# Two indirect gathers for w_out's last two rows a partition, and z computed in rows by 72 matmuls

## The chip, the core and the metric

The kernel runs on one core of a Trainium2 chip. The metric is the device time of one execution in microseconds (us), lower is better. Engines are named as the profile names them: PE (matmuls, with PEld for its weight loads), DVE (vector), ACT (activations and copies), POOL (GpSimd), SP (issues transfers). 16 DMA engines move the data.

## What is computed

One decoding step with one new token. The normalised row goes through attention over a window of 4096 keys and through a gated MLP; both are added to the input.

```
xn = layernorm(x)                                # x: 1 x 576
q  = xn @ wq                                     # 32 heads of 128
k, v = k_cache[:, -4096:], v_cache[:, -4096:]    # 16 heads of 128, each for two heads of q
A  = softmax(q k^T / sqrt(128)) v @ wo           # wo: 4096 x 576

z  = gelu(xn @ w_in)                             # w_in: 576 x 4608
z1, z2 = z[:2304], layernorm(z[2304:])
B  = (z1 * (w_sp * z2 + b_sp)) @ w_out           # w_out: 2304 x 576
out = x + A + B
```

All arrays are bfloat16. Keys, values and weights together are 51 MB, each byte of which is read once.

## The kernel before

**Loads.** SP issues every large load, in a fixed order, into four large buffers that are used in turn (tags a, b, c, d): wq in two parts, K of head groups 0 and 1, w_in in two parts (win, rest), K of group 2, V 0, K 3, V 1, V 2, V 3, then w_out (one load, line 106) and wo in five loads of 14, 9, 6, 2 and 1 rows a partition (line 108). A load waits until the tile that had its buffer before has been read. Four heads make a group; there are four groups. Partition p holds rows 18p to 18p+17 of w_out and 32 rows of wo.

**Order of work.** The order on every engine is written out by hand from line 420 on; nothing is rescheduled. For a group g and half c, `keys(g, c)` transposes the keys with four DVE instructions of 128x1024 (line 258, tile kT), and `scores(g, c)` multiplies them with q (line 265, 16 matmuls into S). `sm_a(g)` takes the maximum (line 286, mx), spreads it over the partitions and lets ACT take the exponential (line 292, pz). `sm_b(g)` transposes the result on DVE (line 303, pt) and copies it with 16 ACT instructions (line 306, PT). `sums(g)` and `pv(g)` are PE's (lines 312 and 329: 32 matmuls with V into ops). `tail(g)` normalises on DVE (rs, om, on), gathers the heads by four matmuls (line 350, yps) and copies them into Y (line 357). From line 426 the calls run: z_mms, sm_b(0), sm_a(1), keys and scores(2,0), sm_b(1), z_exp, keys and scores(2,1), ..., tail(2), sm_b(3), sums(3), pv(3), out_hv(0), out_hv(1), tail(3), out_hv(2), and the products with wo.

**The gated MLP.** `z_mms` (line 360) computes z with the weights as the stationary operand: for each of 9 slices of w_in and each of 18 columns t a weight load of 128x128 and a matmul whose moving operand is XT (two columns, one for each half of z): 162 weight loads and 162 matmuls. The result zps has z in columns: partition p, position t. `z_exp` copies it to SBUF (line 372) and starts the gelu, `z_gelu` ends it, and `z_norm` computes hv, of 18 columns, the factor of w_out; its power (line 404) is POOL's.

**The output.** `acc` has the two parts of the output row (264 and 312 columns) in two banks of PSUM. `out_mms` adds one row a partition of a weight: two matmuls, one for each part, with one column of hv or Y as the stationary operand. `out_hv(c)` does so for six of w_out's 18 rows. Y is complete after tail(3); then the 32 rows of wo follow in order of their loads. DVE and ACT each convert one part (lines 480 and 481), and ACT issues the store.

**Pools that the change touches.** Tag m of ps_m is one PSUM bank that small results use in turn (qps2, lps, psz, yps), so each of them waits until the one before has been read. Tag pt of `single` is the tile of sm_b. The PSUM tags a and b are acc's from line 436 on.

Of the kernel before, what the change touches and what calls it, by code (L numbers as in the profile page):

```python
# [7 lines left out]

FP32 = mybir.dt.float32
BF16 = mybir.dt.bfloat16  # L10
ALU = mybir.AluOpType
ACT = mybir.ActivationFunctionType
AXX = mybir.AxisListType.X

D = 576
# [12 lines left out]
NF = FH // 128  # L28
CUT = (0, 264, D)
XP = D // 3  # L30
EPS = 1e-5
SCALE = DH ** -0.5
GELU_C = 0.7978845608028654
NS = 9


@with_exitstack
def kernel(
# [14 lines left out]
    nc = tc.nc  # L53
    P = nc.NUM_PARTITIONS
# [5 lines left out]
    work = ctx.enter_context(tc.tile_pool(name="work", bufs=2))  # L60
    ktpool = ctx.enter_context(tc.tile_pool(name="ktpool", bufs=2))
    single = ctx.enter_context(tc.tile_pool(name="single", bufs=1))
    ps_s = ctx.enter_context(tc.tile_pool(name="ps_s", bufs=1, space=bass.MemoryType.PSUM))
    ps_o = ctx.enter_context(tc.tile_pool(name="ps_o", bufs=1, space=bass.MemoryType.PSUM))
    ps_m = ctx.enter_context(tc.tile_pool(name="ps_m", bufs=1, space=bass.MemoryType.PSUM))
    ps_a = ctx.enter_context(tc.tile_pool(name="ps_a", bufs=1, space=bass.MemoryType.PSUM))
    ps_b = ctx.enter_context(tc.tile_pool(name="ps_b", bufs=1, space=bass.MemoryType.PSUM))
# [6 lines left out]
    def rows(slot, src, name, lo, n, at=None):  # L74

        w = src.shape[1]
        if at is None:
            t = big.tile([P, n * w], BF16, name=f"{name}{lo}", tag=slot)[:]
        else:
            t = slot[:, at:at + n * w]  # L80
        v = t.rearrange("p (s c) -> p s c", c=w)
        nc.sync.dma_start(v, src.rearrange("(p s) c -> p s c", p=P)[:, lo:lo + n, :])  # L82
        return [(lo + s, v[:, s, :]) for s in range(n)]
# [19 lines left out]
    V[2] = load_kv("b", A_v_cache, 2, "v")  # L103
    V[3] = load_kv("c", A_v_cache, 3, "v")
    ends = [big.tile([P, TP * DH], BF16, name=f"end{n}", tag="ad"[n]) for n in range(2)]
    wout_sb = rows(ends[0], B_w_out, "wout", 0, NF, 0)
    wo_sb = []
    for n, t, at in ((14, 1, 0), (9, 1, 14), (6, 0, NF), (2, 0, NF + 6), (1, 0, NF + 8)):
        wo_sb += rows(ends[t], A_wo, "wo", len(wo_sb), n, at * D)
# [31 lines left out]
    for e in range(2):  # L141
# [5 lines left out]
                            axis=mybir.AxisListType.XY)  # L147
# [17 lines left out]
    for n in range(2):  # L165
        t = ps_s.tile([P, 2, 512], FP32, name=f"S{n}")
# [7 lines left out]
    lx = const.tile([P, NG], FP32, name="lx")  # L174
    mb = const.tile([P, 32], FP32, name="mb")
    nc.gpsimd.memset(mb[:], 0.0)

# [4 lines left out]
    for j in range(NS):  # L182
        nc.tensor.matmul(ps_x[:, j:j + 1], lhsT=xtw[:, j].rearrange("p m h -> p (m h)"), rhs=ones_b[:, 0:1],  # L183
                         start=True, stop=True)
# [6 lines left out]
        out=junk[:], in0=x_col[:], in1=x_col[:], scale=1.0, scalar=0.0,  # L191
# [13 lines left out]
    XT = const.tile([P, NS, 2], BF16, name="XT")  # L205
# [4 lines left out]
    nc.tensor.matmul(ps_x[:, 24:26], lhsT=ones_b[:], rhs=spb[:], start=True, stop=True)  # L210
    wb = const.tile([P, 2], FP32, name="wb")
    nc.vector.tensor_copy(wb[:], ps_x[:, 24:26])


    for s, wv in wq_sb:
        for g in range(4):
            nc.tensor.matmul(  # L217
                qps[32 * g:32 * g + 2, :], lhsT=XT[:, s, :], rhs=wv[:, 512 * g:512 * (g + 1)],
                start=(s == 0), stop=(s == NS - 1), tile_position=(0, 32 * g),
            )  # L220

    q_rep = const.tile([P, 8, 2, 4, 32], BF16, name="q_rep")
# [19 lines left out]
    for a in range(4):  # L242
        for h in range(2):
            for k2 in range(2):
                nc.vector.tensor_scalar_mul(qbv[:, a, h, k2], qpv[:, h, k2], mask4[:, a:a + 1])


    Y = const.tile([P, 32], BF16, name="Y")
    KT = {}
# [2 lines left out]
    def keys(g, c):  # L252

        kT = ktpool.tile([P, TC, 2, 8, GK, 2], BF16, name=f"kT{g}_{c}", tag="kT")
        src = K[g][:, TC * c:TC * (c + 1), :].rearrange("p t d -> p (t d)").bitcast(FP32)
        dst = kT[:].rearrange("p t b r x e -> p (t b r x e)").bitcast(FP32)
        for n in range(4):
            nc.vector.transpose(dst[:, 1024 * n:1024 * (n + 1)], src[:, 1024 * n:1024 * (n + 1)])  # L258
        KT[g, c] = kT

    def scores(g, c):
        kv = KT.pop((g, c))[:].rearrange("p (t s) b r x e -> p b e x t r s", s=2)
        for be in range(4):
            for x in range(GK):
                nc.tensor.matmul(  # L265
                    S[g % 2][32 * x:32 * x + 8, c, :],
                    lhsT=Qb[:, GK * g + x, be].rearrange("p a h -> p (a h)"),
                    rhs=kv[:, be // 2, be % 2, x],
                    start=(be == 0), stop=(be == 3), tile_position=(0, 32 * x),
                )  # L270
# [25 lines left out]
    def sm_b(g):  # L296
        pt = single.tile([P, TC, 32], FP32, name=f"pt{g}", tag="pt")
        src = pz[:].rearrange("p t r x e -> p (t r x e)").bitcast(FP32)
        dst = pt[:].rearrange("p t x -> p (t x)")
        PT = work.tile([P, TC, GK, 2, 2], BF16, name=f"PT{g}", tag="PT")  # L300
        PT4 = PT[:].rearrange("p t x h e -> p (t x h e)").bitcast(FP32).rearrange("p (t x h) -> p t x h", x=GK, h=2)
        for n in range(2):
            nc.vector.transpose(dst[:, 1024 * n:1024 * (n + 1)], src[:, 1024 * n:1024 * (n + 1)])  # L303
        for x in range(GK):
            for a in range(4):
                nc.scalar.copy(PT4[32 * a:32 * a + 32, :, x, :], pt[32 * x:32 * x + 32, :, 2 * a:2 * a + 2])  # L306
        st[g]["PT"] = PT

    def sums(g):

        lps = ps_m.tile([P, 32], FP32, name=f"lps{g}", tag="m")
        nc.tensor.matmul(lps[:, 0:1], lhsT=lsum[:].rearrange("p v y e -> p (v y e)"), rhs=lx[:, g:g + 1],
                         start=True, stop=True)
        st[g]["lps"] = lps
# [43 lines left out]


    def z_mms():  # L360
        zps = ps_a.tile([P, 2, NF], FP32, name="zps", tag="a")
        for s, wv in win_sb:
            wt = wv.rearrange("k (p t) -> k t p", t=NF)
            for t in range(NF):
                nc.tensor.matmul(zps[:, :, t], lhsT=wt[:, t, :], rhs=XT[:, s, :],  # L365
                                 start=(s == 0 and t == 0), stop=(s == NS - 1 and t == NF - 1),
                                 skip_group_check=True)
        return zps

    def z_exp(zps):  # L370
        z = const.tile([P, 2, NF], FP32, name="z")
        nc.vector.tensor_copy(z[:], zps[:])
        u = const.tile([P, 2, NF], FP32, name="u")
        nc.vector.tensor_mul(u[:], z[:], z[:])
        nc.vector.tensor_scalar(out=u[:], in0=u[:], scalar1=0.044715, scalar2=1.0,
                                op0=ALU.mult, op1=ALU.add)
        nc.vector.tensor_mul(u[:], u[:], z[:])
        th = const.tile([P, 2, NF], FP32, name="th")
        nc.scalar.activation(th[:], u[:], ACT.Exp, scale=-2.0 * GELU_C)
        return z, th  # L380
# [15 lines left out]
    def z_norm(G, sz):  # L396
        psz = ps_m.tile([P, 512], FP32, name="psz", tag="m")
        nc.tensor.matmul(psz[:, 0:2], lhsT=ones_f[:], rhs=sz[:], start=True, stop=True)
        mz = const.tile([P, 4], FP32, name="mz")
        nc.vector.tensor_scalar_mul(mz[:, 0:2], psz[:, 0:2], 1.0 / FH)  # L400
        nc.vector.tensor_mul(mz[:, 2:3], mz[:, 0:1], mz[:, 0:1])
        nc.vector.tensor_sub(mz[:, 2:3], mz[:, 1:2], mz[:, 2:3])
        nc.vector.tensor_scalar_add(mz[:, 2:3], mz[:, 2:3], EPS)  # L403
        nc.gpsimd.tensor_tensor(out=mz[:, 3:4], in0=mz[:, 2:3], in1=mhalf[:], op=ALU.pow)  # L404
        zn = const.tile([P, NF], FP32, name="zn")
        nc.vector.tensor_scalar(out=zn[:], in0=G[:, 1], scalar1=mz[:, 0:1], scalar2=mz[:, 3:4],
                                op0=ALU.subtract, op1=ALU.mult)
        nc.vector.tensor_scalar(out=zn[:], in0=zn[:], scalar1=wb[:, 0:1], scalar2=wb[:, 1:2],
                                op0=ALU.mult, op1=ALU.add)
        hv = const.tile([P, NF], BF16, name="hv")  # L410
        nc.vector.tensor_mul(hv[:], G[:, 0], zn[:])
        return hv
# [7 lines left out]
    for g in range(2):  # L420
        for c in range(2):
            keys(g, c)
            scores(g, c)
            if g == 1 and c == 0:
                sm_a(0)
    zps = z_mms()
    sm_b(0)
    sm_a(1)
# [24 lines left out]
    tail(1)  # L453
    sm_a(3)
    hv = z_norm(G, sz)
    sums(2)
    pv(2)
    tail(2)
    sm_b(3)
    sums(3)  # L460
    pv(3)

    def out_mms(lhs, col, wv, last):
        for n in range(2):
            nc.tensor.matmul(acc[n], lhsT=lhs[:, col:col + 1], rhs=wv[:, CUT[n]:CUT[n + 1]],  # L465
                             start=False, stop=last, tile_position=(0, 32 * n))
# [8 lines left out]
    out_hv(2)  # L475
    for t, wv in wo_sb:
        out_mms(Y, t, wv, t == 31)

    res = const.tile([1, D], BF16, name="res")
    nc.vector.tensor_copy(res[:, 0:CUT[1]], acc[0])  # L480
# [32 lines left out]
```

## Time and profile before

| | |
|---|---|
| Time, median of 3 runs (lowest to highest) | 126.92 us (126.77 to 126.95) |
| The profiled execution: its time, its span | 126.89 us, 125.1 us |
| Busy share of the span: PE, PEld, DVE, ACT, POOL | 57%, 23%, 63%, 34%, 6% |
| SP's queue: packets, data, share of 16 DMA engines | 2592, 50.96 MB, 95.2% |
| z: 126 + 36 matmuls on PE | 48.82 to 56.79 and 56.66 to 59.03 us |
| Last part of wo issued, then landed, as the chain of waits has it | 90.41 us, 121.27 us |
| Conversion of the result on ACT | 122.72 to 123.13 us |

The span runs from the first to the last instruction that the profile shows; the time of an execution has 1.8 us more around it. Times in the text are us from the start of the span. A line of the timeline has the start, the length, the engine, the line of code, the operation, the tiles written and read with their shapes, and the number of instructions put together; in brackets stands how long the engine was idle before and what ended that. A queue's line has its packets, megabytes, and the time of its packets as a share of 16 engines' span. The queue called q1 is SP's, q10 is ACT's, and q8 and q14 bring instructions to the engines.

### The profile page before, as it was taken

Reading aid. Unit: us, or ns where it says so; the run is one execution under the profiler, and the core shown is the slowest. Engines: PE = TensorE matmul, PEld = TensorE weight load, DVE = VectorE, ACT = ScalarE, POOL = GpSimd, SP = SyncE. Lnnn points to the kernel's source line nnn. Section 1 sums busy time; section 2 is a strip of 40 time slices with the busy share of each in tenths; the row PEclk is TensorE's granted clock in tenths of the full one; section 3 lists DMA queues with packets and bytes.
Section 4 is the critical chain, followed back from the end, with each engine's and each line's share of the span. In section 5 each row is a group of like instructions: output and inputs, shape, how many; then the busy total and the mean of one; then the engine's idle time right before and its main releaser. Section 6 shows DMA issues by size and latency. Waiting matters only on the chain.

```text
span 125.1 us, 1617 instructions
## 1 busy us (share of the span) xinstructions
PE 70.8 (57%) x626; PEld 28.9 (23%) x626; DVE 78.5 (63%) x150; ACT 43.2 (34%) x101; POOL 7.1 (6%) x19
## 2 busy tenths in 40 slices
PE   0012841009878469998390992059892932049992
PEld 0001201001101013998000131002211411015850
DVE  6745025899799976308999367999938359003301
ACT  2100011000000956996069008707801941940001
POOL 2961000000000000000000000000000100000000
PEclk9999998555995867755559599657998555555899
DMA  4999899998999999898999989999999999999960
GB/s 118 511 422 440 385 471 440 398 492 356 487 420 402 385 493 461 377 492 372 461 451 398 482 367 477 401 451 430 409 482 398 451 394 440 418 413 416 428 237 0
DMA packets 2611, 51.06 MB, mean 408 GB/s; under 512 B 299, under 2 KB 428, under 8 KB 684
## 3 DMA queue, kind: packets, MB, share of 16 engines
q1 hardware_dynamic: 2592, 50.96, 95.2%
q8 instruction: 5, 0.08, 0.2%
q14 instruction: 2, 0.02, 0.0%
q10 hardware_dynamic: 12, 0.00, 0.0%
HBM read 50.96 MB, written 0.00 MB: 407 GB/s over the span
## 4 chain that ended last, share of the span: by engine, by line
DMA 61%; DVE 30%; PE 5%; SPq 1%; issue 1%; ACT 0%; DVEq 0%
DMA k<-in_A_k_cache_dram 37%; DMA end<-in_A_wo_dram 25%; DVE kT L258 22%; DVE pt L303 4%; PE S L265 3%; PE acc L465 1%; SPq L82 1%; DVE mx L286 1%; DVE on L343 1%; DVE om L339 1%; PE yps L350 0%; ACT res L481 0%; DVE rs L320 0%; DVE mt L275 0%; DVE mb L281 0%
## 5 line engine op out<-in xcount | busy, mean ns | idle before, releaser
L265 PE MATMUL S<-kT,Qb 128*8 128x512 bf16 x128 | 32.5, 1148 | 23.3 <-DVE kT L258 22.8
L258 DVE STREAM_TRANSPOSE kT<-k 128x1024 f32<-128x1024 f32 x32 | 36.8, 1207 | 6.5 <-DMA k<-in_A_k_cache_dram 6.5
L292 ACT ACTIVATE pz<-S,nm 32x1024 bf16<-32x1024 f32 x16 | 19.1, 1192 | 33.6 <-DVE nm L289 20.6
L306 ACT COPY PT<-pt 32x128 f32<-32x128 f32 x64 | 19.8, 309 | 17.2 <-DVE pt L303 16.5
L329 PE MATMUL ops<-v,PT 128*32 128x512 bf16 x128 | 11.0, 505 | 6.8 <-ACT PT L306 6.8
L265 PEld LDWEIGHTS <-Qb 128*8 128x8 bf16 x128 | 3.5, 96 | 45.0 <-issue 34.8
L303 DVE STREAM_TRANSPOSE pt<-pz 128x1024 f32<-128x1024 f32 x8 | 9.4, 1210 | 0.8 <-ACT pz L292 0.8
L339 DVE SCALAR_TENSOR_TENSOR om<-ops,rs,dmask 128x512 f32<-128x512 f32 x4 | 3.0, 750 | 10.5 <-PE ops L329 10.3
L365 PEld LDWEIGHTS <-win 128*128 128x128 bf16 x126 | 7.9, 165 | 1.9 <-issue 1.9
L365 PE MATMUL zps<-XT,win 128*128 128x2 bf16 x126 | 8.0, 202 | 0.0
L286 DVE TENSOR_REDUCE mx<-S 128x1 f32<-128x1024 f32 x4 | 4.9, 1214 | 3.9 <-PE S L265 3.9
L329 PEld LDWEIGHTS <-PT 128*32 128x32 bf16 x128 | 3.7, 117 | 11.5 <-ACT PT L306 6.9
L226 ACT CAST q_rep<-qps 128x512 bf16<-128x512 f32 x2 | 1.2, 586 | 14.9 <-DVE q_rep L228 14.9
L404 POOL TENSOR_TENSOR mz<-mz,mhalf 128x1 f32<-128x1 f32 x1 | 0.6, 554 | 85.5 <-DVE mz L403 85.5
L183 PE MATMUL ps_x<-ones_b,xtw 1*128 1x1 bf16 x9 | 0.4, 162 | 8.7 <-DVE xtw L181 8.7
L465 PE MATMUL acc<-end,Y 128*1 128x312 bf16 (+1 forms) x64 | 4.9, 285 | 0.3 <-DMA end<-in_A_wo_dram 0.3
L228 DVE CAST q_rep<-qps 128x512 bf16<-128x512 f32 x2 | 1.4, 692 | 5.1 <-PE qps L217 4.5
L481 ACT CAST res<-acc 1x312 bf16<-1x312 f32 x1 | 0.4, 411 | 11.7 <-PE acc L465 11.7
L350 PE MATMUL yps<-on,sel 128*32 128x32 f32 x32 | 2.0, 210 | 4.1 <-DVE on L343 4.1
L343 DVE TENSOR_REDUCE on<-om 128x128 f32<-128x512 f32 x4 | 4.2, 1042 | 0.1
L480 DVE CAST res<-acc 1x264 bf16<-1x264 f32 x1 | 0.4, 420 | 5.2 <-PE acc L465 5.2
L465 PE MATMUL acc<-end,hv 128*1 128x264 bf16 (+1 forms) x36 | 3.6, 360 | 0.0
(92 smaller groups left out, 56.6 us busy)
## 6 DMA issues: line engine op xcount, KB each, us to landing
k<-in_A_k_cache_dram SPq DMA_DIRECT2D x4, 4096.0 KB
v<-in_A_v_cache_dram SPq DMA_DIRECT2D x4, 4096.0 KB, 26.0
win<-in_B_w_in_dram SPq DMA_DIRECT2D x1, 4032.0 KB, 27.1
wq<-in_A_wq_dram SPq DMA_DIRECT2D x1, 3584.0 KB, 12.8
end<-in_B_w_out_dram SPq DMA_DIRECT2D x1, 2592.0 KB, 22.3
end<-in_A_wo_dram SPq DMA_DIRECT2D x1, 2016.0 KB
end<-in_A_wo_dram SPq DMA_DIRECT2D x1, 1296.0 KB
rest<-in_B_w_in_dram SPq DMA_DIRECT2D x1, 1152.0 KB
```

What stands on the lines that cost most here:

```text
L258: nc.vector.transpose(dst[:, 1024 * n:1024 * (n + 1)], src[:, 1024 * n:1024 * (n + 1)])
L265: nc.tensor.matmul(S[g % 2][32 * x:32 * x + 8, c, :], lhsT=Qb[:, GK * g + x, be].rearrange("p a h -> p (a h)"), rhs=kv[:, be // 2, be % 2, x],
L286: nc.vector.tensor_reduce(out=mx[:, 0:1], in_=s[:], op=ALU.max, axis=mybir.AxisListType.XY)
L292: nc.scalar.activation(pz[lo:hi, :, :, x, :], s[lo:hi].rearrange("p a (t r e) -> p (a t) r e", r=8, e=2), ACT.Exp, bias=nm[lo:hi, 0:1], sc ...
L303: nc.vector.transpose(dst[:, 1024 * n:1024 * (n + 1)], src[:, 1024 * n:1024 * (n + 1)])
L306: nc.scalar.copy(PT4[32 * a:32 * a + 32, :, x, :], pt[32 * x:32 * x + 32, :, 2 * a:2 * a + 2])
L329: nc.tensor.matmul(ops[32 * q:32 * q + 32, :], lhsT=d["PT"][:, t0 // 2:t0 // 2 + 2].rearrange("p t x h e -> p (t x h e)"), rhs=V[g][:, t0: ...
L339: nc.vector.scalar_tensor_tensor(out=om[:].rearrange("p c d -> p (c d)"), in0=ops[:], scalar=d["rs"][:, 0:1], in1=dmask[:].rearrange("p c ...
L343: nc.vector.reduce_sum(on[:], om[:].rearrange("p c d -> p d c"), axis=AXX)
L350: nc.tensor.matmul(yps[32 * g:32 * g + 32, :], lhsT=sel[:, dq, :], rhs=d["on"][:, 32 * dq:32 * dq + 32], start=(dq == 0), stop=(dq == 3), ...
L365: nc.tensor.matmul(zps[:, :, t], lhsT=wt[:, t, :], rhs=XT[:, s, :], start=(s == 0 and t == 0), stop=(s == NS - 1 and t == NF - 1), skip_gr ...
L465: nc.tensor.matmul(acc[n], lhsT=lhs[:, col:col + 1], rhs=wv[:, CUT[n]:CUT[n + 1]], start=False, stop=last, tile_position=(0, 32 * n))
```

## The change

It has two parts.

**w_out's last two rows a partition by gathers.** SP's load of w_out takes 16 of 18 rows a partition. The other two (2,304 bytes, contiguous in memory) are read by two indirect DMAs that POOL issues (`load_ext`). For these, w_out is seen as 1152 pairs of rows; partition p needs pair 9p+8. The first gather has the index 9p+8 for all partitions except 40, whose index is 4096; an index over 1151 is skipped, and the tile `ext` keeps the zeros that it was set to. The second gather reads the 40 pairs left out, into 40 other partitions, and skips the others. The 40 skipped partitions are 20 to 27, 52 to 59, 84 to 91, 116 to 123, 68 to 71 and 100 to 103, which the change names as those of DMA engines 5, 6, 13, 14 and 9; the partitions that receive are 60 to 67, 72 to 79, 92 to 99, 104 to 111, 28 to 31 and 124 to 127, named as those of 7, 8, 10, 11 and 15.

The indices are computed on the way: POOL builds them as diagonals of two 128x128 tiles (in the buffer of tag pt), PE adds these up into a column (`pick`), DVE converts it (`rows_to_take`, behind the transposes of keys(0,0)). POOL also builds `move`, a permutation by which one matmul brings the last two columns of hv from the skipped partitions to the receiving ones (`hx_ps`, copied to `hx` by DVE, between sm_b(3) and sums(3)). The gathers are issued behind z_norm. The eight matmuls for both halves of `ext` (two rows with hv and two with hx) stand behind t = 13 of wo; out_hv(2) has four rows instead of six.

**z in rows.** The stationary operand is now XZ (XT with 30 columns of zeros), the moving one the weights: 9 slices x 2 halves of t x 4 quarters of the partitions, 72 matmuls of 288 columns, each into 32 partitions of one of two PSUM tiles. z lies in rows of 32 there, so z_exp transposes both tiles on DVE, into the space of q_rep, and copies z out of it.

```diff
+SPARED = ((20, 8), (52, 8), (84, 8), (116, 8), (68, 4), (100, 4))
+GIVEN = (60, 72, 92, 104, 28, 124)
...
-    wout_sb = rows(ends[0], B_w_out, "wout", 0, NF, 0)
+    wout_sb = rows(ends[0], B_w_out, "wout", 0, NM, 0)
...
+    gap.tile([P, 176], BF16, name="unused")
+    ext = far.tile([P, 2, NX, D], BF16, name="ext")
...
+    move = more.tile([P, P], BF16, name="move")
+    nc.vector.memset(move[:], 0.0)
+    XZ = more.tile([P, NS, 32], BF16, name="XZ")
+    nc.vector.memset(XZ[:], 0.0)
+    nc.vector.tensor_copy(XZ[:, :, 0:2], XT[:])
+    nc.vector.memset(ext[:], 0.0)
...
+    for (lo, n), at in zip(SPARED, GIVEN):
+        nc.gpsimd.tensor_copy(move[:, at:at + n], ident[:, lo:lo + n])
+    both = single.tile([P, 4, P], FP32, name="both", tag="pt")
+    which = []
+    for g in range(2):
+        col = both[:, 2 * g].bitcast(I32)
+        if g == 0:
+            nc.gpsimd.iota(col, pattern=[[PAIRS, P]], base=PAIRS - 1, channel_multiplier=0)
+            for lo, n in SPARED:
+                nc.gpsimd.memset(col[:, lo:lo + n], FAR)
+        else:
+            nc.gpsimd.memset(col, FAR)
+            for (lo, n), at in zip(SPARED, GIVEN):
+                nc.gpsimd.iota(col[:, at:at + n], pattern=[[PAIRS, n]], base=PAIRS * lo + PAIRS - 1, channel_multiplier=0)
+        diag = both[:, 2 * g + 1]
+        nc.gpsimd.tensor_copy(diag, col)
+        nc.gpsimd.tensor_tensor(out=diag, in0=diag, in1=ident[:], op=ALU.mult)
+        which.append(diag)
+
+    pick = ps_m.tile([P, 2], FP32, name="pick", tag="m")
+    for g, diag in enumerate(which):
+        nc.tensor.matmul(pick[:, g:g + 1], lhsT=diag, rhs=ones_f[:, 0:1], start=True, stop=True)
+
+    def rows_to_take():
+        idx = more.tile([P, 2], I32, name="idx")
+        nc.vector.tensor_copy(idx[:], pick[:])
+        which[:] = [idx[:, g:g + 1] for g in range(2)]
+
+    def load_ext():
+        pairs = B_w_out.rearrange("(r s) c -> r (s c)", s=NX)
+        for g in range(2):
+            nc.gpsimd.indirect_dma_start(
+                out=ext[:, g].rearrange("p s c -> p (s c)"), out_offset=None, in_=pairs,
+                in_offset=bass.IndirectOffsetOnAxis(ap=which[g], axis=0),
+                bounds_check=P * PAIRS - 1, oob_is_err=False)
...
     def z_mms():
-        zps = ps_a.tile([P, 2, NF], FP32, name="zps", tag="a")
+        zps = [pool.tile([P, ZT, 32], FP32, name=f"zps{n}", tag="ab"[n]) for n, pool in enumerate((ps_a, ps_b))]
         for s, wv in win_sb:
-            wt = wv.rearrange("k (p t) -> k t p", t=NF)
-            for t in range(NF):
-                nc.tensor.matmul(zps[:, :, t], lhsT=wt[:, t, :], rhs=XT[:, s, :],
-                                 start=(s == 0 and t == 0), stop=(s == NS - 1 and t == NF - 1),
-                                 skip_group_check=True)
+            wt = wv.rearrange("k (q p t) -> k q t p", q=4, t=NF)
+            for n in range(2):
+                for q in range(4):
+                    nc.tensor.matmul(zps[n][32 * q:32 * q + 32], lhsT=XZ[:, s, :], rhs=wt[:, q, ZT * n:ZT * (n + 1), :],
+                                     start=(s == 0), stop=(s == NS - 1), tile_position=(0, 32 * q))
         return zps
...
-        nc.vector.tensor_copy(z[:], zps[:])
+        zt = q_rep[:].rearrange("p m b a d -> p (m b a d)").bitcast(FP32)[:, 0:32 * NF]
+        for n in range(2):
+            nc.vector.transpose(zt[:, 32 * ZT * n:32 * ZT * (n + 1)], zps[n][:].rearrange("p t c -> p (t c)"))
+        nc.vector.tensor_copy(z[:], zt.rearrange("p (t c) -> p t c", c=32)[:, :, 0:2].rearrange("p t h -> p h t"))
...
+            if g == 0 and c == 0:
+                rows_to_take()
...
     hv = z_norm(G, sz)
+    load_ext()
     sums(2)
     pv(2)
     tail(2)
     sm_b(3)
+    hx_ps = ps_m.tile([P, 32], FP32, name="hx_ps", tag="m")
+    nc.tensor.matmul(hx_ps[:, 0:NX], lhsT=move[:], rhs=hv[:, NM:NF], start=True, stop=True)
+    hx = more.tile([P, NX], BF16, name="hx")
+    nc.vector.tensor_copy(hx[:], hx_ps[:, 0:NX])
     sums(3)
     pv(3)
...
         out_mms(Y, t, wv, t == 31)
+        if t == 13:
+            for j in range(NX):
+                out_mms(hv, NM + j, ext[:, 0, j, :], False)
+                out_mms(hx, j, ext[:, 1, j, :], False)
```

Here NX = 2, NM = 16, PAIRS = 9, FAR = 4096 and ZT = 9. `gap` keeps 352 bytes a partition free ahead of `ext`.

More of the change, by code (lines that the diff above doesn't have):

```diff
@@ L10 @@
 BF16 = mybir.dt.bfloat16
+I32 = mybir.dt.int32
 ALU = mybir.AluOpType
@@ L30 @@
 XP = D // 3
+NX = 2
+NM = NF - NX
+PAIRS = NF // NX
+FAR = 4096
+SPARED = ((20, 8), (52, 8), (84, 8), (116, 8), (68, 4), (100, 4))
+GIVEN = (60, 72, 92, 104, 28, 124)
 EPS = 1e-5
@@ L34 @@
 NS = 9
+ZT = NF // 2
 @with_exitstack
@@ L62 @@
     single = ctx.enter_context(tc.tile_pool(name="single", bufs=1))
+    gap = ctx.enter_context(tc.tile_pool(name="gap", bufs=1))
+    far = ctx.enter_context(tc.tile_pool(name="far", bufs=1))
+    more = ctx.enter_context(tc.tile_pool(name="more", bufs=1))
     ps_s = ctx.enter_context(tc.tile_pool(name="ps_s", bufs=1, space=bass.MemoryType.PSUM))
```

## The prediction

> **What bounds the kernel now.** I read the busy shares in slices and the queues first, then the end of the transfers in narrow stretches, then the timeline backwards from the result to the last long wait. From the page:
>
> ```profile
> DMA  4999899998999999898999989999999999999960
> ...
> q1 hardware_dynamic: 2592, 50.96, 95.2%
> q8 instruction: 5, 0.08, 0.2%
> ```
>
> The 16 DMA engines are busy from start to end; SP's queue alone fills 95.2% of their span. So bytes set a floor. The end of that floor, in stretches (columns: stretch, its length, busy PE, PEld, DVE, ACT, POOL, granted clock, DMA share, GB/s):
>
> ```profile
> 120.00:120.20 0.20, 0.20 (x6) 0.11 (x4) 0.00 (x0) 0.00 (x0) 0.00 (x0) 1.00 0.98 375
> ...
> 121.60:121.80 0.20, 0.20 (x8) 0.20 (x5) 0.00 (x0) 0.00 (x0) 0.00 (x0) 1.00 0.22 75
> ```
>
> At 120.1 all 16 engines work, at 121.7 about 0.22 x 16 = 3.5 do. Put one behind the other, the trace's packets end on ten engines at 120.09 to 120.56 us, on two at 120.86 and 120.96, on four at 121.74 to 122.00. The late ones had instruction packets in between: q8's packets start at 36.47, 57.16, 77.70 and 100.96, take 0.94 us each, and the data packet behind each takes 0.5 us longer, 1.4 us in all. So there is something to level: at most about 1 us.
>
> But compute ends at nearly the same time. The timeline from the last wait of DVE for data:
>
> ```profile
> 56.69 4.62 DVE L258 STREAM_TRANSPOSE kT<-k 128x1024 f32<-128x1024 f32 x4 [5.44 <-DMA k<-in_A_k_cache_dram]
> ...
> 63.49 0.16 DVE L372 COPY z<-zps 128x36 f32<-128x36 f32 x1
> ...
> 64.24 4.62 DVE L258 STREAM_TRANSPOSE kT<-k 128x1024 f32<-128x1024 f32 x4
> ...
> 68.91 4.02 PE L265 MATMUL S<-kT,Qb 128*8 128x512 bf16 x16 [3.41 <-DVE kT L258]
> ```
>
> After 56.69 DVE never again waits for a transfer. Its work is one chain with PE and ACT: kT(2,0), pt(1) from 61.23 to 63.56, z, kT(2,1), S, mx (from 72.98, where S ends) and the small steps to Y(0) at 78.18; kT(3,0), pt(2), kT(3,1) to 89.47; S to 93.45; Y(1), mx(3), mz; the PV matmuls of group 2 from 97.14 to 100.74; Y(2) at 103.5; pt(3); 16 ACT copies to 110.99; PV of group 3; Y(3). In each of these steps the next one starts within 0.4 us of the one before. The end:
>
> ```profile
> 111.04 3.60 PE L329 MATMUL ops<-v,PT 128*32 128x512 bf16 x32 [6.81 <-ACT PT L306]
> ...
> 117.30 0.20 DVE L357 CAST Y<-yps 32x32 bf16<-32x32 f32 x1 [0.78 <-PE yps L350]
> ...
> 117.77 3.26 PE L465 MATMUL acc<-end,Y 128*1 128x264 bf16 x44
> 121.31 1.36 PE L465 MATMUL acc<-end,Y 128*1 128x264 bf16 x18 [0.28 <-DMA end<-in_A_wo_dram]
> ```
>
> Y(3) is there at 117.50. From then PE runs 64 matmuls for w_o at 3.26 / 44 = 74 ns each and waits for data only once, 0.28 us. So the floor of the bytes and the chain of compute lie 0.28 us apart, and **what is added to compute beyond 0.28 us is paid in full.**
>
> **Part by part.** *Transfers.* The w_out load loses 2,304 of 20,736 bytes a partition. Its packets take 771 ns, so 771 x 2304 / 20736 = 86 ns less, times 8 packets an engine: 0.69 us. A gathered row has the size of a 2304-byte w_o packet, which took 93 ns; 8 of them take 0.74 us. If the four late engines are among the skipped, they end at 121.05 to 121.3; engines that give and take their own rows end 0.05 later; receivers 0.8 later, 120.9 to 121.4 if they are of the ten. The transfers would then end about 0.6 us earlier. This is worth nothing while PE is the later one (below), and 0.6 us if that cover is gone.
>
> The gather itself has no row in this trace. Its packets could cost as little as 93 ns each between others (the 384-byte packets of the x load cost their engine about 25 ns), or as much as the extra that follows an instruction packet (0.5 us) on each of 16 rows of a receiver, 8 us. I take 93 ns, since source and target are those of ordinary loads; the top is a rival. It is issued on POOL behind L404's power (97.17 to 97.72 now), with nothing queued behind it. ext is first read by the 29th w_o matmul, at about 120.5, 22 us later.
>
> *z in rows, on PE.* 162 matmuls with 162 weight loads (7.97 + 2.37 = 10.3 us, from 48.82 to 59.03) become 72 of 288 columns. No row has this shape. Lower bound: the q matmuls, 28 of 512 columns in 3.16 us, so 63 ns for 288 columns, 4.6 us. Upper bound: S, whose columns are strided too, 16 in 4.09 us, 144 ns for 288, 10.4 us. I take S's. PE is next needed at 61.37, so nothing of it is on the path; 2.3 us more than that bound would be.
>
> *z in rows, on DVE.* This is on the path, between pt(1) and kT(2,1). Two transposes of 128x288 from PSUM are added. A 128x32 one takes 0.21 us (L275) and a 128x1024 one 1.19 (L303), so 0.99 ns a column, 0.46 us for 288; the pair at L303 takes 2.33 in all, so two overlap by 0.05: 0.87 us. The copy to z takes its 0.16 as before, but starts 0.03 behind its input where now it overlaps. Sum **+0.90 us**. Below: kT's 4.62 / 4096 columns, 0.65. Above: PSUM at the 1.35 ns a column of L228's casts, 1.05. Late by as much are kT(2,1), S, and all of the chain.
>
> *The end on PE.* out_hv(2) loses four matmuls before Y(3), and eight are put behind t = 13 of w_o: 8 x 74 ns = **+0.59**. The four came while PE waited for Y(3), except some 0.07 us that ran into w_o's first: **-0.07**. The one wait for data goes: **-0.28**.
>
> *At no cost.* Three memsets and a copy on DVE behind L212 (about 1.6 us, the largest by L167's 0.91 for as many words) fall into DVE's wait of 4.48 us for q; without it they would delay q_rep. The 24 small operations on POOL cost 0.12 to 0.55 each by L173 and L404, 2.9 to 13.2 us, and end at 14.6 to 24.9; the pick matmuls that need them stand before S(0,0), which waits for kT until 28.33. The idx copy (0.16) delays kT(0,1), and DVE's wait of 0.69 at 33.47 and of 5.44 at 56.69 swallow it. hx (one matmul, one 0.16 copy) comes at about 106, and lps of group 3 waits for it; PE stands idle there until 111.04 for ACT's copies.
>
> *Sum.* 0.90 + 0.59 - 0.07 - 0.28 = +1.14 us. The profiled execution took 126.89 (span 125.1 and 1.8 around it), 0.03 under the median of 126.92. 126.89 + 1.14 = **128.0 us**. With the bounds of the transposes and 0.2 either way at the end: 127.6 to 128.4.
>
> **Rivals.** *The clock gives it back.* PV of groups 0 and 1 ran at a granted clock of 1.00, of groups 2 and 3 at 0.50 (same columns as above):
>
> ```profile
> 99.00:100.00 1.00, 1.00 (x16) 0.32 (x8) 0.00 (x0) 0.97 (x3) 0.00 (x0) 0.50 1.06 459
> ...
> 74.00:75.00 1.00, 1.00 (x28) 0.43 (x16) 0.86 (x5) 0.00 (x0) 0.00 (x0) 1.00 0.92 393
> ```
>
> It took 3.60 us there and 1.91 here, and it is on the chain each time. If the shifted work gets the full clock in one of the slow ones, the chain is 1.7 us shorter, 0.55 shorter than now, and the transfers decide: 0.6 earlier at best, **126.3 us**. It decides from 1.14 us on. For it: grants change in steps of 3.41 us, and work shifted by 0.9 falls otherwise into them. Against: before PV of group 3 PE idles from 104.2 to 111.04, and the shift does not change that; and the full clock of groups 0 and 1 can be lost as well, 1.7 us the other way. The Trainium skill, "TensorE: Matmul & The Clock Gate", Part 1, says that the gate judges by free-running windows of about 3.4 us, so that the same kernel meets them otherwise from run to run. The trace agrees on the length; that the four times of before lie within 0.18 us speaks against much of it here. By that rule this rival and its opposite are about as likely.
>
> *The gather comes late.* If a gathered packet waits for two data packets instead of one, a receiver's 16 take 16 x (2 x 0.69 + 0.09) = 23.5 us from about 101, so 124.5, and PE stands from 120.5 before ext: about 4 us more, **132 us**. It decides when ext lands after 120.5. Against: instruction and x packets slipped in among a full queue of SP. The Trainium skill, "DMA: Bandwidth & Descriptors", section "Queues, rings and completion order", says that an engine takes turns between queues packet by packet; by that rule 16 x 0.78 = 12.5 us, landing at about 113.5, and no wait.
>
> *K of group 2 comes earlier.* DVE's start at 56.69 hangs on the one engine that the first instruction packet held up for 1.4 us; the second latest engine ended that load 0.9 us earlier. If the packet falls elsewhere, DVE's +0.90 is paid from its own wait: 126.89 + 0.24 = **127.1 us**. For it: PE's program is shorter. Against: PE's program before 36.47 only gains the few pick instructions.
>
> *It does not relieve the late engines* (other engines are late than the skipped ones): the transfers end at 122.0 or up to 0.8 later. PE is then still the later one by this sum; no change to 128.0.
>
> **How the numbers follow.** Forecast, with the last rival in it, 0.74; clock 0.12; gather late 0.06; K earlier 0.08. What can be told from no change is 0.2%, 0.25 us. Slower: forecast 0.73, gather 0.06 and 0.02 of K earlier, 0.81. Same: 0.06 of K earlier and 0.01, 0.07. Faster: 0.12. The range takes in K earlier and a part of the clock's shifts upward: 127.0 to 128.6.
>
> **What would show it.** Right: behind pt(1) two transposes at about 0.46 us and kT(2,1) starting about 7.6 + 0.9 us after kT(2,0) did; Y(3) near 118.4; then 72 matmuls without a wait for data, to about 123.8, with the DMA share at zero before 121.8. Wrong: a wait of PE for end or ext in the last 5 us; PV of group 2 or 3 in 1.9 us; kT(2,0) starting before 56.2; z's matmuls still running at 61.4.

## The result, and the profile after

| | before | after |
|---|---|---|
| Time, median (lowest to highest), 22 executions each | 126.88 us (126.66 to 127.09) | 127.68 us (126.40 to 128.23) |
| Ratio of the times, 95% interval | | 1.0046 [1.0027, 1.0065] |
| The profiled execution: its time, its span | 126.89 us, 125.1 us | 126.47 us, 124.5 us |

The changed kernel is slower by 0.8 us in the median. But its executions spread over 1.8 us where those of before spread over 0.43: eight took 126.40 to 127.38 us, fourteen 127.64 to 128.23. The profile shows one of the eight, in fact the second fastest of all. What it shows must be read as that execution, not as the median.

From the page after, the DMA share in slices and the queues:

```profile
DMA  4999899998989899998989999898999999999980
...
q1 hardware_dynamic: 2592, 50.66, 95.2%
q0 software_dynamic: 160, 0.30, 0.6%
q8 instruction: 4, 0.07, 0.2%
```

SP's queue moves 0.30 MB less, the new queue q0 (the gathers) moves them, in 0.6% of the 16 engines' span. That is 0.006 x 16 x 124.5 = 12 us in all. In the trace's packets it is 64 of 4,608 bytes, two rows each, at 178 ns (89 ns a row), and 96 of 4 or 8 bytes at 9 ns. From the timeline after:

```profile
56.59 4.62 DVE L313 STREAM_TRANSPOSE kT<-k 128x1024 f32<-128x1024 f32 x4 [4.65 <-DMA k<-in_A_k_cache_dram]
...
63.39 0.81 DVE L429 STREAM_TRANSPOSE q_rep<-zps 128x288 f32<-128x288 f32 x2
...
64.23 0.20 DVE L430 COPY z<-q_rep 128x36 f32<-128x36 f32 x1
...
65.02 4.62 DVE L313 STREAM_TRANSPOSE kT<-k 128x1024 f32<-128x1024 f32 x4
...
97.81 1.91 PE L384 MATMUL ops<-v,PT 128*32 128x512 bf16 x32
...
110.03 3.47 PE L384 MATMUL ops<-v,PT 128*32 128x512 bf16 x32 [4.22 <-ACT PT L361]
...
115.91 0.20 DVE L412 CAST Y<-yps 32x32 bf16<-32x32 f32 x1 [0.53 <-PE yps L405]
...
120.58 1.38 PE L530 MATMUL acc<-end,Y 128*1 128x264 bf16 x18 [0.68 <-DMA end<-in_A_wo_dram]
```

The second half of the keys of group 2 starts 8.43 us after the first, before 7.55: DVE's chain takes 0.88 us more there, as forecast. But PV of group 2 (97.81) has 1.91 us, where it had 3.60. The granted clock in it was 0.50 before (the prediction shows the line); here it is 1.00:

```profile
99.00:100.00 1.00, 0.72 (x16) 0.11 (x6) 0.83 (x5) 0.99 (x2) 1.00 (x1) 1.00 1.22 524
```

Mostly for this, Y(3) is done at 116.11, 1.39 us earlier than before instead of 0.9 later, and at the end PE waits for wo. The end of the transfers, in stretches (columns as in the prediction):

```profile
120.00:120.20 0.20, 0.00 (x0) 0.00 (x0) 0.00 (x0) 0.00 (x0) 0.00 (x0) 1.00 0.95 340
...
121.00:121.20 0.20, 0.20 (x8) 0.20 (x5) 0.00 (x0) 0.00 (x0) 0.00 (x0) 1.00 0.42 144
...
121.60:121.80 0.20, 0.20 (x5) 0.08 (x1) 0.00 (x0) 0.00 (x0) 0.00 (x0) 1.00 0.00 0
```

Before, 3.5 engines worked at 121.7; here none does. Put one behind the other, the packets end on the 16 engines at 119.75 to 121.29 us, before at 120.09 to 122.00. In this execution the change does to the transfers what it says, 0.7 us of it.

### The profile page after: what moved, and what is told of

Read it like the earlier page. It is cut to its first block, busy times and chain, and to the rows that moved or that the text cites. A ratio compares the mean times of both kernels' runs of the same rounds, so it can differ in the third digit from the quotient of the medians.

```text
span 124.5 us, 1494 instructions
## 1 busy us (share of the span) xinstructions
PE 69.1 (55%) x545; PEld 21.6 (17%) x545; DVE 80.9 (65%) x158; ACT 43.2 (35%) x101; POOL 12.7 (10%) x45
## 4 chain that ended last, share of the span: by engine, by line
DMA 60%; DVE 31%; PE 5%; SPq 1%; issue 1%; ACT 0%; DVEq 0%
DMA k<-in_A_k_cache_dram 37%; DMA end<-in_A_wo_dram 23%; DVE kT L313 22%; DVE pt L358 4%; PE S L320 3%; DVE om L394 1%; PE acc L530 1%; SPq L93 1%; DVE mx L341 1%; DVE on L398 1%; DVE q_rep L429 1%; PE yps L405 0%; ACT res L550 0%; DVE rs L375 0%; DVE mt L330 0%
## 5 line engine op out<-in xcount | busy, mean ns | idle before, releaser
L384 PE MATMUL ops<-v,PT 128*32 128x512 bf16 x128 | 9.8, 460 | 4.2 <-ACT PT L361 4.2
L421 PE MATMUL zps<-win,XZ 128*32 128x288 bf16 x56 | 7.4, 693 | 0.0
L530 PE MATMUL acc<-end,Y 128*1 128x264 bf16 (+1 forms) x64 | 4.8, 285 | 0.7 <-DMA end<-in_A_wo_dram 0.7
L367 PE MATMUL lps<-lx,lsum 128*128 128x1 f32 x8 | 1.9, 304 | 4.8 <-DVE hx L524 2.7
L530 PEld LDWEIGHTS <-Y 128*1 128x1 bf16 x64 | 3.4, 83 | 1.9 <-issue 1.4
```

Source lines behind the costliest of these rows:

```text
L384: nc.tensor.matmul(ops[32 * q:32 * q + 32, :], lhsT=d["PT"][:, t0 // 2:t0 // 2 + 2].rearrange("p t x h e -> p (t x h e)"), rhs=V[g][:, t0: ...
L421: nc.tensor.matmul(zps[n][32 * q:32 * q + 32], lhsT=XZ[:, s, :], rhs=wt[:, q, ZT * n:ZT * (n + 1), :], start=(s == 0), stop=(s == NS - 1), ...
```

## The experiments

Three questions: what does z in rows cost alone, why is the clock of this execution higher, and what puts more than half of the executions at 127.6 to 128.2. The kernel before was timed beside each: 126.95 to 127.03 us in the median. "Packets end" is always read as above, from the packets of one engine put one behind the other.

### z in rows alone

```diff
-    wout_sb = rows(ends[0], B_w_out, "wout", 0, NM, 0)
+    wout_sb = rows(ends[0], B_w_out, "wout", 0, NF, 0)
...
-    load_ext()
...
-        if t == 13:
-            for j in range(NX):
-                out_mms(hv, NM + j, ext[:, 0, j, :], False)
-                out_mms(hx, j, ext[:, 1, j, :], False)
```

(against the changed kernel; everything that serves the gathers is gone with it)

> The kernel before with z in rows only, no gathers. Theory (compute chain): the two transposes put 0.87 us on DVE's chain, of which PE's wait of 0.28 us at the end swallows a part: about +0.6 us, 127.4 to 127.5, with single runs down to 126.9 (the transfers' floor, unchanged) when PV of group 2 gets the full clock. Rival (the gathers are what costs, by POOL's descriptors or by their packets): no change, 126.9.

Measured: 127.20 us (126.96 to 127.54, 12 executions), ratio 1.0021 [1.0008, 1.0033]: 0.23 us slower, half of what was expected. Its timeline:

```profile
98.13 3.60 PE L334 MATMUL ops<-v,PT 128*32 128x512 bf16 x32
...
118.05 0.20 DVE L362 CAST Y<-yps 32x32 bf16<-32x32 f32 x1 [0.53 <-PE yps L355]
...
118.39 4.53 PE L473 MATMUL acc<-end,Y 128*1 128x264 bf16 x64
```

With PV at half clock as before, Y(3) is 0.75 us later than before. But the 64 matmuls of wo then run through in 4.53 us, 71 ns each, without a wait; in the trace of before they took from 117.55 to 122.69, 5.14 us. So not 0.28 but 0.61 us of waiting lay in them, only part of it in the one gap that the timeline names. What landed at 121.27 there was not the last part of wo: the 18 matmuls behind that gap read the parts of 6, 2 and 1 rows a partition, and the packets of the last part ran to 122.00. PE's last weight load waited for that one, too:

```profile
122.38 0.08 PEld L465 LDWEIGHTS <-Y 128*1 128x1 bf16 x1 [0.17 <-issue]
```

With z in rows alone PE ends at 122.92, 0.23 later than before, and that is the measured difference.

### The same, with z's DVE work behind the scores

```diff
-    zg = z_exp(zps)
     keys(2, 1)
     scores(2, 1)
+    zg = z_exp(zps)
```

> z in rows only, no gathers, with z's DVE work behind kT(2,1), where DVE waits for S. Theory (what z in rows costs is its 0.87 us on DVE's chain): compute ends 0.7 us earlier than in the kernel before, the transfers decide: no change, 126.9, against 127.2 with z in its old place. Rival (z in rows costs on PE or elsewhere): 127.2.

Measured: 126.93 us (126.76 to 127.19, 11 executions), ratio 0.9999 [0.999, 1.0008]; 0.27 us less than with z's work ahead of the keys.

```profile
63.54 4.58 DVE L263 STREAM_TRANSPOSE kT<-k 128x1024 f32<-128x1024 f32 x4
...
68.04 0.81 DVE L379 STREAM_TRANSPOSE q_rep<-zps 128x288 f32<-128x288 f32 x2
68.18 4.02 PE L270 MATMUL S<-kT,Qb 128*8 128x512 bf16 x16 [2.74 <-DVE kT L263]
...
72.25 1.22 DVE L291 TENSOR_REDUCE mx<-S 128x1 f32<-128x1024 f32 x1 [1.05 <-PE S L270]
```

The transposes and all of the gelu now lie in DVE's wait for S (68.18 to 72.20), and mx starts 0.73 us earlier than before the change. The 0.88 us of DVE were all of the cost of z in rows that shows in the time, and behind the scores they cost nothing.

### PE kept busy ahead of PV of group 2

```diff
     hv = z_norm(G, sz)
+    for n in range(6):
+        nc.tensor.matmul(banks[0][64:96, :], lhsT=ident[:, 0:32], rhs=Qb[:].rearrange("p m b a h -> p (m b a h)"),
+                         start=True, stop=True, tile_position=(0, 64))
```

(with z in rows alone, z's work ahead of the keys; the six matmuls write a part of a PSUM bank that nothing reads)

> z in rows only, no gathers, z in its old place, and six matmuls of 512 columns without use between psz and lps of group 2, where PE is idle for 2.1 us before PV of group 2. Theory (PV of group 2 runs at half clock only because PE idles before it): PV of group 2 takes 1.9 instead of 3.6 us, compute ends 1.7 us earlier, the transfers decide: 126.9 in every run, against 127.2. Rival (the clock does not follow PE's idle time): 3.6 us or more, 127.2 or slower.

Measured: 126.99 us (126.84 to 127.26, 11 executions), ratio 1.0002 [0.9993, 1.0011].

```profile
95.36 1.47 PE L466 MATMUL acc<-Qb,ident 128*32 128x512 bf16 x6
...
97.83 1.91 PE L334 MATMUL ops<-v,PT 128*32 128x512 bf16 x32
```

1.47 us of idle matmuls ahead of it, and PV takes 1.91 us instead of 3.60. Y(3) came at 116.28 us and PE waited for wo, so of the 1.7 us gained only 0.21 reach the time: the transfers, whose packets end at 121.91, decide. This is one trace, and PV of group 2 takes 1.91 us in the profiled execution of the changed kernel without any idle matmul, and 2.88 to 3.61 in the others, so part of it may be luck; that all eleven executions stay at or under 127.26, where z in rows alone goes to 127.54, fits the expectation. The Trainium skill, "TensorE: Matmul & The Clock Gate", Part 1, has the gate judge PE's activity in windows of about 3.4 us; the traces agree on the length, their grants change in steps of 3.41 us.

### The gathers alone

```diff
-        zps = [pool.tile([P, ZT, 32], FP32, name=f"zps{n}", tag="ab"[n]) for n, pool in enumerate((ps_a, ps_b))]
+        zps = ps_a.tile([P, 2, NF], FP32, name="zps", tag="a")
...
-                    nc.tensor.matmul(zps[n][32 * q:32 * q + 32], lhsT=XZ[:, s, :], rhs=wt[:, q, ZT * n:ZT * (n + 1), :],
-                                     start=(s == 0), stop=(s == NS - 1), tile_position=(0, 32 * q))
+                nc.tensor.matmul(zps[:, :, t], lhsT=wt[:, t, :], rhs=XT[:, s, :],
+                                 start=(s == 0 and t == 0), stop=(s == NS - 1 and t == NF - 1),
+                                 skip_group_check=True)
```

> The kernel after with z in columns as before, gathers kept. Theory (compute chain): DVE's chain is as before, PE has eight matmuls more behind Y(3), 0.59 us, less the 0.28 us wait and 0.07: about +0.25 us, 127.1; single runs down to 126.3, where PV of group 2 gets the full clock and the transfers, 0.6 to 0.7 us shorter, decide. Rival (the gathers are what costs): all of the loss stays, 127.7.

Measured: 127.62 us, ratio 1.0037 [1.001, 1.0065]. That median describes no execution: six took 126.44 to 127.35 us and six 127.90 to 128.12. No part of the forecast made room for the second six. The kernels with z in rows and no gathers have none over 127.54 in 34 executions. So the second group comes with the gathers. Its profiled execution (127.19 us) is of the first group: PE reads ext from 119.35 on, where the last packet of the gathers ended at 110.40, and runs to the end without a wait.

### The extra matmuls early

```diff
     sums(3)
+    for j in range(NX):
+        out_mms(hv, NM + j, ext[:, 0, j, :], False)
+        out_mms(hx, j, ext[:, 1, j, :], False)
     pv(3)
...
-        if t == 13:
-            for j in range(NX):
-                out_mms(hv, NM + j, ext[:, 0, j, :], False)
-                out_mms(hx, j, ext[:, 1, j, :], False)
```

> The kernel after with the eight matmuls of ext moved from behind t = 13 of w_o to ahead of PV of group 3, where PE waits for ACT. Theory: 8 x 74 ns leave the end of PE, 0.5 to 0.6 us less than after: about 127.1, single runs 126.3. Rival (the gathers cost as transfers, or ext lands after 111): 127.7 or more, with PE waiting for ext.

Measured: 127.34 us (127.06 to 128.29), ratio 1.0032 [1.0012, 1.0051]. Eight of 12 took 127.06 to 127.40, within the range of z in rows alone; the other four took 127.56 to 128.29. But the move is not free, since PE now waits for ext (profiled execution, 127.31 us):

```profile
108.30 0.42 PE L529 MATMUL acc<-ext,hv 128*1 128x264 bf16 x2 [1.13 <-DMA ext<-in_B_w_out_dram,idx]
...
111.32 0.42 PE L529 MATMUL acc<-ext,hx 128*1 128x264 bf16 x2 [2.60 <-DMA ext<-in_B_w_out_dram,idx]
```

ACT's copies end at 111.35 there, and PE's matmuls for PV share the next microsecond with those for ext: DVE can use the result of PV 4.38 us after the last copy, with z in rows alone 3.7. So this run does not show what the eight matmuls cost at the end. An estimate for the changed kernel is the range of z in rows alone (126.96 to 127.54) with 8 x 71 ns = 0.57 us added, 127.5 to 128.1; its fourteen lie at 127.64 to 128.23.

### Both moves

The edits of the last kernel and of z's work behind the scores together; run twice, on two chips.

> As the run before, and z's DVE work (transposes, copy, u) moved behind kT(2,1), where DVE waits 2.9 to 3.2 us for S. Theory: compute ends 0.7 us earlier than in the kernel before, the transfers decide in every run: 126.2 to 126.4, narrow. Rival (the gathers cost as transfers): 127 or more. Rival (z's place does not matter): as the run before, 127.1.

> The run with ext early and z hidden once more, unchanged, beside the next one on one chip. Theory (receivers 7, 8, 10, 11, 15 are held up in about half of the executions): both groups again, 126.5 to 127.3 and 127.6 to 128.1. Rival (the slow group belonged to the chip that this kernel ran on before): one group only.

Measured: 127.78 us (126.61 to 128.03), ratio 1.0044 [1.0019, 1.0069]; the second time 127.84 (126.56 to 128.13), 1.0048 [1.0025, 1.0072]. Ten of the 24 executions took 126.56 to 127.25 us, fourteen 127.65 to 128.13. The expectation of one narrow group near 126.3 failed. The end of the two profiled executions, 126.81 and 126.56 us:

```profile
117.11 3.21 PE L529 MATMUL acc<-end,Y 128*1 128x264 bf16 x46
120.74 1.56 PE L529 MATMUL acc<-end,Y 128*1 128x264 bf16 x18 [0.42 <-DMA end<-in_A_wo_dram]
```

```profile
117.59 4.48 PE L529 MATMUL acc<-end,Y 128*1 128x264 bf16 x64
```

In the first, PE waits for wo at the end. In the second nothing waits, though PE starts 0.48 us later: packets end at 121.41, and PE runs 64 matmuls through to 122.07: 126.56 us. Compute alone allowed 126.6 there, and yet more than half of the executions are 1.1 to 1.5 us longer.

Here, too, compute hangs on the gathers by way of ext. In the second profiled execution:

```profile
110.57 0.42 PE L529 MATMUL acc<-ext,hx 128*1 128x264 bf16 x2 [3.65 <-DMA ext<-in_B_w_out_dram,idx]
```

ACT's last copy ended at 109.67, and PV of group 3 started behind ext, at 110.60. A second gather that lands later still would make this kernel slower through PE, without a late end of wo.

The mean granted clock, which is known for every execution, does not tell the groups apart: 0.768 to 0.836 in the ten, 0.769 to 0.847 in the fourteen.

### Gathers without other receivers

```diff
-SPARED = ((20, 8), (52, 8), (84, 8), (116, 8), (68, 4), (100, 4))
-GIVEN = (60, 72, 92, 104, 28, 124)
+SPARED = ()
+GIVEN = ()
```

(with both moves; one gather, in which every partition takes its own rows, and no hx)

> The run with ext early and z hidden, but with one gather that brings every partition its own two rows; no engine is spared and none gets more. Theory (the engines that instruction packets hold up are not the same in every execution, and the slow times, 127.6 to 128.0, are those in which a held-up engine also receives the others' rows): the late engines end about 0.05 us later than in the kernel before, whichever they are: one narrow group at 126.9 to 127.1, neither 126.6 nor 127.9. Rival (a gather by POOL is itself slow in some executions): the group at 127.9 stays.

Measured: 127.03 us, ratio 1.0012 [0.9995, 1.0029]; eleven of 12 lie at 126.85 to 127.22, one at 128.23, which stays unexplained. In stretches:

```profile
121.60:121.80 0.20, 0.20 (x9) 0.20 (x5) 0.00 (x0) 0.00 (x0) 0.00 (x0) 1.00 0.18 63
```

Three engines still work at 121.7, as before the change; four end at 121.63 to 122.02. The gather as such shows no cost, and the second group is nearly gone with the shift of rows between engines. One more thing differs from both moves: without the second gather ext is there early, and PV of group 3 starts at 110.28, as soon as ACT's copies end. The experiments below keep both gathers.

### The roles swapped

```diff
-SPARED = ((20, 8), (52, 8), (84, 8), (116, 8), (68, 4), (100, 4))
-GIVEN = (60, 72, 92, 104, 28, 124)
+SPARED = ((60, 8), (72, 8), (92, 8), (104, 8), (28, 4), (124, 4))
+GIVEN = (20, 52, 84, 116, 68, 100)
```

(with both moves)

> The run with ext early and z hidden, with the roles swapped: 7, 8, 10, 11, 15 are spared, 5, 6, 9, 13, 14 receive. Theory (held-up engines differ between executions): the profiled execution, in which 5, 6, 9, 13, 14 seem to be the held-up ones, is now a slow one, near 127.8, with late ends at about 122.7 and 16 gathered rows on each late engine; other executions are faster, down to 126.6. Rival (held-up engines are always the same): every run is slow, 127.7 to 127.9. Rival (the gathers are slow by themselves): times as without the swap, both groups, the profiled one near 126.8.

Measured: 127.95 us (127.86 to 128.38, 6 executions), ratio 1.0085 [1.0071, 1.0099].

```profile
121.98 1.45 PE L529 MATMUL acc<-end,Y 128*1 128x264 bf16 x18 [0.71 <-DMA end<-in_A_wo_dram]
```

```profile
122.40:122.60 0.20, 0.20 (x8) 0.20 (x5) 0.00 (x0) 0.00 (x0) 0.00 (x0) 1.00 0.14 46
```

Four engines end at 122.44 to 122.76, 0.7 later than before the change; followed back through the trace's packets, three of them carry eight packets of the gathers, as only a receiver does. PE starts its last 18 matmuls at 121.98 instead of 121.31. So the engines named 5, 6, 9, 13 and 14 do hold the late ones, and a receiver that is late anyway gives 127.9 to 128.4: the times of the second group. If in about half of the executions other engines were the late ones, the swap would have been short in those; in six, none was.

### Other receivers

```diff
-GIVEN = (60, 72, 92, 104, 28, 124)
+GIVEN = (0, 32, 8, 40, 16, 48)
```

(with both moves; by the naming of the change, engines 0 to 4 receive. Run twice, the second time on the same chip as the second run of both moves)

> The run with ext early and z hidden; 5, 6, 9, 13, 14 spared as there, but 0, 1, 2, 3, 4 receive (partitions 0 to 19 and 32 to 51). Theory (in some executions instruction packets hold up engines that receive): the slow group at 127.6 to 128.0 has the share of executions in which one of 0 to 4 is held up, which may differ from the 7 of 12 with 7, 8, 10, 11, 15; executions in which only engines that neither give nor receive are late stand at 127.0; the profiled one near 126.7. Rival (moving rows by gathers is slow in some executions, whichever engines receive): again about 7 of 12 at 127.6 to 128.0.

> The run with receivers 0 to 4 once more, unchanged, on the same chip as the run before. Theory: one group, 126.9 to 127.5, whatever the chip. Rival (the slow group belongs to the chip): the same groups as the run before.

Measured: 127.15 us (126.95 to 127.48, 11 executions), ratio 1.0013 [1.0003, 1.0022], and 127.09 (126.79 to 127.21, 11 executions), 1.0007 [0.9996, 1.0017]. One group both times: none of 22 over 127.48, where with the old receivers 14 of 24 are. Nothing but the receivers differs. But it is not faster than before either: in the profiled executions packets go on to 121.85 and 121.82 us, and the engine that ends last carries eight packets of the gathers, so it is a receiver here, too. PE waits for ext as with the old receivers (up to 110.47 in the first), so that wait alone does not make the second group.

```profile
121.60:121.80 0.20, 0.20 (x8) 0.15 (x3) 0.00 (x0) 0.00 (x0) 0.00 (x0) 1.00 0.11 40
```

### Other engines spared

```diff
-SPARED = ((20, 8), (52, 8), (84, 8), (116, 8), (68, 4), (100, 4))
+SPARED = ((0, 8), (8, 8), (32, 8), (40, 8), (16, 4), (48, 4))
```

(with both moves; engines 0 to 4 give, 7, 8, 10, 11 and 15 receive as in the change)

> The run with ext early and z hidden; 7, 8, 10, 11, 15 receive as there, but 0, 1, 2, 3, 4 are spared. Theory: the slow group hangs on the receivers alone, so about half of the executions stand at 127.6 to 128.0 again; the others at 126.9 to 127.1, since 5, 6, 9, 13, 14 are not relieved; none at 126.6. The profiled one is near 127.0, with late ends at about 122.0 and eight gathered rows on each late engine. Rival (the relief of 5, 6, 9, 13, 14 is not what made the fast executions): some at 126.6 again.

Measured: 127.37 us (127.11 to 128.06, 8 executions), ratio 1.0038 [1.0016, 1.0059]; five took 127.11 to 127.39 and three 127.86 to 128.06. The end of the profiled execution (127.33 us):

```profile
121.45 1.37 PE L529 MATMUL acc<-end,Y 128*1 128x264 bf16 x18 [0.69 <-DMA end<-in_A_wo_dram]
```

Packets end up to 122.16: the late engines keep their rows, so the first group is at the time of before or a little over it. The second group is there again. It goes with the receivers 7, 8, 10, 11 and 15, whichever engines are spared.

## Why the prediction was right, and where it was not

The time came out near the forecast, 127.68 us against 128.0. The one execution of the changed kernel that has a trace does not show the forecast's path: it has two of the signs that were named for being wrong, PV of group 2 in 1.91 us and a wait of PE for end in the last 5 us. The terms are therefore read from this trace one by one, and from the other kernels.

**DVE's chain** ("+0.90 us"): right. The two transposes took 0.81 us; kT(2,1) starts 0.88 later behind kT(2,0) than before, and mx 0.87 later in the span; the kernel that hides the transposes behind S gives all of its cost back.

**z's matmuls on PE** ("I take S's", 144 ns): right, 132 to 141 ns, done at 58.83 us and hidden.

**The gather's packets** (93 ns): right in size, 89 ns a row, though two rows go in one packet. POOL issued the gathers at 98.92 and 100.49 us, they landed about 10 us later, and PE did not wait for ext. The packets of two rows lie between 103.34 and 110.23; a receiver's eight, each behind one packet of w_out, would take 8 x (0.69 + 0.18) = 6.9 us by an estimate from their lengths, which fits. The rival of the late gather (132 us) is out: no execution of any kernel is over 128.38. *K of group 2 earlier* did not happen in this execution: kT(2,0) started at 56.59, 0.10 earlier than before.

**The end on PE** ("what is added to compute beyond 0.28 us is paid in full"): right mechanism, mis-sized term. The slack was 0.61 us, since PE also waited for the last part of wo, which the table of the times before has as landed at 121.27, and the 74 ns that were taken for a matmul had waiting in them; without it they take 71. By the prediction's own terms z in rows alone would cost 0.90 - 0.28 = 0.62 us; it cost 0.23. With that and 8 x 71 ns - 0.07 the sum becomes 126.88 + 0.23 + 0.57 - 0.07 = 127.6 us, against a measured median of 127.68. The lesson is in the reading: a wait that is named once in a row of matmuls need not be the only one, and the rate of a stretch that ends at a transfer is not the engine's rate.

**The clock gives it back** (126.3 us, at 0.12): it happened in the profiled execution, with PV of group 2 in 1.91 us and the transfers deciding at 126.47. The kernel that keeps PE busy makes it likely, by one trace, that PE's activity ahead of PV is what grants it. How often the changed kernel gets it is not known, since only one execution has a trace and the mean clock is 0.816 both in the eight shorter executions and in the fourteen longer ones.

**It does not relieve the late engines** ("the transfers end at 122.0 or up to 0.8 later. PE is then still the later one by this sum; no change to 128.0"): this is the step that fell short. It treats the late engines as one set that is either hit or missed. In the trace after, in that of the gathers alone and in both of those with both moves, the set is hit: no engine works at 121.6 to 121.8 us. With both moves and a PE that can end at 126.6, 14 of 24 executions took 127.65 us or more; with nothing changed but the receivers, none of 22 did. So in over half of the executions the time is some 1.1 us longer (127.94 against 126.88, the medians of the two groups), and it hangs on the receivers. There are two ways for that: the receivers' own last packets of wo come late, or, in the kernels with ext early, their gathered rows do, and PV of group 3 with them. With the gathers alone ext is read some 9 us after its last packet in the trace, and six of 12 executions are at 127.90 to 128.12 all the same, so ext cannot be the whole of it. That the transfers of wo are then the later ones is inferred from this and from the swap; no trace shows it. Twelve of the fourteen lie at 127.9 to 128.13, the time of the roles swapped, where a held-up engine also receives.

The two mechanisms, 127.6 by compute and 127.9 by a late receiver, lie close together in the changed kernel. Thirteen of its fourteen longer executions took 127.64 to 127.89 us and one 128.23, which fits compute better than a late receiver; in how many a receiver was late as well, is not shown. That the forecast of 128.0 is near the median is partly luck: with compute that allowed 126.6, the kernel with both moves has nearly the same median (127.78 and 127.84), for a reason that is not in the sum.

**What stays open.** The number of late engines goes with the instruction packets: before, q8 has four ahead of the last microseconds, and four engines end late; with z in rows and no gathers it has three, and three engines end late (121.80 to 121.94) in each of the three kernels. That does not tell which engine is late in the second group. No execution of the second group has a trace, and the records of packets carry no engine number, so which of 7, 8, 10, 11 and 15 is late, and by what, is not shown. One reading is that one of them is held up as by an instruction packet: 121.3 + 1.4 = 122.7, near the 122.76 of the roles swapped. That the instruction packets simply move to other engines is the weaker form of it, since the swap then should have been short at times. The other reading is a rule: the Trainium skill, "DMA: Bandwidth & Descriptors", section "Latency and other measured facts", says that engines 7 and 15 are usually slower than the others in traces and suspects the descriptors of transfers issued by software, which these gathers are (their queue is called software_dynamic). Both engines are among the receivers, and neither is among 0 to 4. The gathers of own rows, which use 7 and 15 without a surplus, had one long execution in 12; that neither bears the rule out nor refutes it, since four engines end at 121.63 to 122.02 us there, and one that ended at 121.1 could be 0.9 us later unseen. Receivers 8, 10 and 11 alone would have told the two apart; that was not tried.

No version beat the kernel before. The nearest are z in rows with its DVE work behind the scores (0.9999 [0.999, 1.0008]) and the other receivers with both moves (1.0007 [0.9996, 1.0017]).

## What to carry to other kernels

A load that is balanced engine by engine after one profiled execution is balanced for that execution: look at all the times first, and where they fall into two groups, ask what differs between executions before trusting the trace. Work added to an engine costs its length only on the chain that ends last; 0.88 us of DVE was free four instructions further on, inside a wait for PE. And the slack at a shared end is found by what the later engine does when nothing makes it wait, not by the one wait that is named.

## What was not expected of the hardware

The same kernel has two groups of times, 126.6 to 127.3 and 127.7 to 128.1 us, on each of two chips, and a list of receiving partitions removes the second.

With six idle matmuls of 1.47 us, placed so that PE is at work ahead of PV, PV took 1.69 us less (1.91 instead of 3.60, one trace of each).

Gathered rows of 2304 bytes, issued by POOL into the middle of a full queue of SP, cost their engine no more than SP's own packets of that size: 178 ns for a packet of two, 89 a row, against 93.
